# Gated mix of attention and a mixture of experts on one core: weights of the output projection fetched by another queue, and small work given other pairs of key tiles

## The chip, the cores and the metric

The kernel runs on one core of a Trainium2 chip. The core has engines that work side by side: TensorE (PE, with its weight loads shown as PEld), VectorE (DVE), ScalarE (ACT), GpSimd (POOL) and SyncE (SP, which here does nothing but issue DMAs). Each takes its instructions in order and waits on semaphores for the others. The metric is the device time of one execution in microseconds (us), less is better. "Faster" and "slower" are meant against the kernel before, on the same chip.

## The reference

One input x (2048 rows of D = 448) goes through full attention and through a mixture of experts, and a learned gate mixes the two:

```
qkv = x @ wqkv                      # 16 heads of 28
p   = softmax(q @ k.T * 28**-0.5)   # all 2048 keys, no mask
A   = (p @ v).reshape(S, D) @ wo
B   = sum over the top 2 of 8 experts of gate_e * (silu(x @ w1[e]) @ w2[e])
out = g * A + (1 - g) * B           # g per row, from gate_w
```

All is float32; the kernel computes the products of the projections and scores from two float32r parts, high and low ("h", "l"), of each factor.

## The kernel before

The projections, the router and the experts come first, until about 830 us. The rest is attention and the output projection, and only these are changed. Attention runs over 16 units. Unit u = 4g + qc takes group g of four heads and block qc of 512 queries, and goes over the keys in 8 pairs p of key tiles (128 keys each); m = 8u + p counts the pairs. For each m the code issues, in this order: `scores(m + 1)` (the scores of the next pair on TensorE, their exponentials on ScalarE), `beside(m)` (loads and small work that is spread over the pairs) and `values(m)` (P times V on TensorE).

On PE, DVE, ACT and POOL the instructions keep the order in which the code is written (`manual_schedule`). SP's queue is ordered by a scheduler, and comes out in the written order here. Of the two key tiles of a pair the scores of each fill three banks of one PSUM tile (`s0`, `s1`) and one single bank (`z0`, `z1`). The single banks are used in turn by the scores and by `values`; the last score bank of a pair is copied to SBUF by DVE (`X`, L1168), so that the bank is free again. `values` writes its result `po` into such a bank too, and DVE copies it to `osb` in pair 0 (L1185) or adds it to `osb` in the other pairs (L1187). `osb` is `accs[u]`, one tile per unit, in a pool with two buffers. Row 28 of each head's 32 rows of `osb` is the sum of the exponentials, since V carries a column of ones.

The small work beside this, with its lines before the change:

- `load_q(g, qc)` (L719, L721): 12 DMAs on SP that fetch the queries of the next unit, called in `scores(m)` where a unit begins. `load_k` (L704, L707: eight for `Kh`, four for `Kl`) and `load_v` (L691) fetch half of the keys or values of the next group; in the last unit of a group (qc = 3) they are called in pairs 3, 4 and 6, the second half of V in pair 0 of the next.
- `split_wo(b)` (L1051 to L1053): fetches block b of the output projection's weights wo into `wo_r` by a DMA of POOL and splits it on DVE into `wo_h` and `wo_l`.
- `fetch_routed(t)` and `routed(t)` (L1059, L1068 to L1072): gather the experts' rows of 128 tokens by two indirect DMAs of POOL and form the weighted sum B in four steps on DVE.
- `collect_sums(u)`, `invert_sums(u)`, `divide(u)` (L1105 to L1130): POOL sends the sums of exponentials to DRAM (`sum_d`) and fetches them back in another layout (`rc`), DVE inverts them, POOL sends them out again (`inv_d`) and spreads them over the partitions (`rs`), and DVE multiplies `osb` with them (L1120). Then SP moves the rows of `osb` to their places in `OT` (L1130): four DMAs for units 0 to 3, five for units 4 to 11 and eight for units 12 to 15.
- `split_o(t, eng)`: splits a token tile of OT into `oh` and `ol` for the output projection, which follows over 16 token tiles (`project`, `finish`).

## Time and profile before

| | us |
|---|---|
| median of 3 runs | 1383.28 (1382.78 to 1384.16) |
| the profiled execution, its time | 1384.45 |
| its span (first to last instruction) | 1382.7 |
| TensorE matmuls busy | 1348.1 (98%) |
| VectorE busy | 927.5 (67%) |
| ScalarE busy | 847.5 (61%) |
| GpSimd busy | 618.5 (45%) |

The granted clock of TensorE is 0.99 of full speed on average. The profile is one execution; its times below are counted from the start of its span. In the list of waits a row reads: engine, what it was about to write and in which line, what it waited for, the total of the waits in us, their number, the longest. A row of the timeline reads: start, duration, engine, line, operation, and in brackets the idle time before it and who ended it. SPq and POOLq are the issue of DMAs by these engines.

### The profile page before, as it was taken

The numbers are of one execution on the slowest core, as the hardware profiler recorded it, in microseconds if no ns is written. First come the engines' busy times: TensorE is split into PE (matmuls) and PEld (weight loads), VectorE is DVE, ScalarE is ACT, GpSimd is POOL, SyncE is SP. The second block draws the span as 40 slices with busy tenths as digits, with TensorE's granted clock in tenths as the row PEclk, the third lists the DMA queues.
The fourth block names the chain that finished last, engine by engine and source line by source line (L and its number), as shares of the span: only waits on it lengthen the run. The fifth ranks groups of instructions, "written<-read, shape, count | busy, mean of one in ns | idle before, by whom it ended". The sixth has DMA issues, their size and how long they took to land. (4 is left out here: it accounts for less than half of the span.)

```text
span 1382.7 us, 27175 instructions
## 1 busy us (share of the span) xinstructions
PE 1348.1 (98%) x10166; PEld 891.0 (64%) x10166; DVE 927.5 (67%) x1077; ACT 847.5 (61%) x1269; POOL 618.5 (45%) x665
## 2 busy tenths in 40 slices
PE   9999999999999999999999999999889989999998
PEld 8888788788877777777777774444333334444457
DVE  5736898888888989889887773444433444444555
ACT  5335355355344443444434349999888779999981
POOL 2114676577568675787767550222222112222220
PEclk9999999999999999999999999999999999999999
DMA  9887865653454454553445212225221322242223
GB/s 353 295 288 235 305 178 168 220 170 96 148 161 142 119 160 153 173 157 115 155 146 173 73 38 74 60 61 164 63 63 56 113 71 76 86 127 60 68 59 113
DMA packets 135958, 191.30 MB, mean 138 GB/s; under 512 B 23284, under 2 KB 102168, under 8 KB 135312
## 3 DMA queue, kind: packets, MB, share of 16 engines
q1 hardware_dynamic: 124416, 159.63, 36.7%
q0 software_dynamic: 11264, 29.68, 6.9%
q8 instruction: 80, 1.31, 0.4%
q14 instruction: 54, 0.44, 0.1%
q10 hardware_dynamic: 144, 0.23, 0.1%
HBM read 139.20 MB, written 60.74 MB: 145 GB/s over the span
## 5 line engine op out<-in xcount | busy, mean ns | idle before, releaser
L143 DVE TENSOR_REDUCE mp<-pm 128x3 f32<-128x1536 f32 (+1 forms) x301 | 508.7, 1732 | 11.0 <-PE pm L122 11.0
L1181 PE MATMUL z<-P,V 128*32 128x512 f32 x2032 | 249.4, 608 | 0.5 <-ACT P L1166 0.3
L733 PE MATMUL z<-Q,Kh 29*128 29x512 f32 x508 | 187.6, 448 | 24.4 <-DVE osb L1187 24.4
L1169 ACT ACTIVATE P<-s 128x1536 f32<-128x1536 f32 x127 | 196.2, 1545 | 22.4 <-PE s L733 22.4
L1167 ACT ACTIVATE P<-s 128x1536 f32<-128x1536 f32 x127 | 194.9, 1535 | 0.1
L1168 DVE COPY X<-z 128x512 f32<-128x512 f32 x127 | 87.8, 691 | 154.7 <-PE z L733 145.4
L733 PE MATMUL s<-Q,Kh 29*128 29x512 f32 x1524 | 189.4, 446 | 0.0
L804 POOL TENSOR_TENSOR w2l<-w2r,w2h 128x448 fp32r<-128x448 f32 x112 | 129.3, 1155 | 119.0 <-ACT w2h L798 92.4
L1020 ACT ACTIVATE yo<-acc 128x448 f32<-128x448 f32 x64 | 34.8, 544 | 233.2 <-PE acc L1006 220.5
L1006 PE MATMUL acc<-w2h,hh 128*128 128x448 f32 x448 | 167.6, 374 | 0.3 <-PEq L818 0.3
L1006 PE MATMUL acc<-w2h,hl 128*128 128x448 f32 x448 | 166.5, 372 | 0.0
L1006 PE MATMUL acc<-w2l,hh 128*128 128x448 f32 x448 | 166.1, 371 | 0.0
L733 PEld LDWEIGHTS z<-Q,Kh 29*128 29x128 f32 x508 | 75.3, 185 | 134.0 <-issue 30.5
L949 ACT ACTIVATE hf<-acc 128x512 f32<-128x512 f32 (+6 forms) x154 | 74.2, 482 | 137.9 <-PE acc L945 130.9
L136 DVE TENSOR_REDUCE mp<-acc 128x1 f32<-128x512 f32 x130 | 89.4, 688 | 87.1 <-PE pm L122 85.5
L813 POOL TENSOR_TENSOR hl<-hf,hh 128x512 fp32r<-128x512 f32 x112 | 144.9, 1294 | 1.0 <-ACT hh L952 1.0
L1105 POOL DMA_DIRECT2D sum_d<-osb x64 | 31.0, 492 | 254.5 <-DVE osb L1187 254.5
L1181 PEld LDWEIGHTS z<-P,V 128*32 128x32 f32 x2032 | 53.9, 110 | 133.3 <-issue 81.2
L945 PE MATMUL acc<-xeh,w1h 128*128 128x512 f32 (+3 forms) x408 | 136.8, 339 | 0.0
L945 PE MATMUL acc<-xeh,w1l 128*128 128x512 f32 (+3 forms) x408 | 136.0, 338 | 0.0
L1187 DVE TENSOR_TENSOR osb<-z,osb 128x512 f32<-128x512 f32 x112 | 77.4, 691 | 83.4 <-PE z L1181 81.0
L772 POOL TENSOR_TENSOR w1l<-w1r,w1h 128x1024 fp32r<-128x1024 f32 (+1 forms) x49 | 90.9, 1855 | 64.5 <-ACT w1h L766 47.8
(222 smaller groups left out, 2782.4 us busy)
## 6 DMA issues: line engine op xcount, KB each, us to landing
w2r<-in_w_dram SPq DMA_DIRECT2D x112, 224.0 KB
w1r<-in_w_dram SPq DMA_DIRECT2D x56, 384.0 KB
ys_d<-zero_d SPq DMA_DIRECT2D x32, 448.0 KB
ys_d<-yo SPq DMA_DIRECT2D x64, 224.0 KB
x_d<-xf SPq DMA_DIRECT2D x115, 64.0 KB
qkh_d<-hi SPq DMA_DIRECT2D x28, 256.0 KB
qkl_d<-lo SPq DMA_DIRECT2D x28, 256.0 KB
w1r<-in_w_dram SPq DMA_DIRECT2D x112, 64.0 KB
```

What stands on the lines that cost most here:

```text
L136: nc.vector.tensor_reduce(mp[:, o:o + 1], banks[0], axis=AX.X, op=ALU.max)
L143: nc.vector.tensor_reduce(mp[:, (o + lo) % 256:(o + lo) % 256 + hi - lo], pm[h][:, lo - 3 * h:hi - 3 * h], axis=AX.X, op=ALU.max)
L733: nc.tensor.matmul(banks[j], k[rw, ks], q[rw, c], start=i == 0, stop=i == 2)
L772: nc.gpsimd.tensor_tensor(l[:, :, half], r[:, :, half], h[:, :, half].bitcast(F32), op=ALU.subtract)
L804: nc.gpsimd.tensor_tensor(w2l, w2r, w2h.bitcast(F32), op=ALU.subtract)
L813: nc.gpsimd.tensor_tensor(hl, hf32, hh[:, 0:512].bitcast(F32), op=ALU.subtract)
L945: nc.tensor.matmul(pu[:, 0:HC], a, b[:, cs], start=i == 0, stop=i == len(mms) - 1)
L1006: nc.tensor.matmul(py[:n, 0:D], a[:, cs], b, start=i == 0, stop=i == 3 * NH - 1)
L1167: nc.scalar.activation(P[:, 1:4], t[0], AF.Exp, scale=SCALE)
L1168: nc.vector.tensor_copy(X, z[1])
L1169: nc.scalar.activation(P[:, 4:7], t[1], AF.Exp, scale=SCALE)
L1181: nc.tensor.matmul(po[32 * j:32 * j + 32], v[:, kt % 8, 32 * j:32 * j + 32], P[4 * i + j], start=i == 0, stop=i == 1)
```

## The change

The fetch of wo leaves `split_wo` and becomes `fetch_wo`, on SP, in pair 4 of units 4 to 7; the split follows in pair 0 (before: pair 1) of units 5 to 8. `collect_sums(u - 1)` is called at the beginning of `beside` for pair 0 of unit u, where it stood at the end of `values` for the last pair of unit u - 1. The gather goes from pair 0 to pair 1, the four steps of the routed rows from pairs 3, 4, 6, 7 to pairs 2, 4, 5, 6, the inversion from pair 2 to pair 3, the spreading of the inverted sums gets a function of its own in pair 4, and the division goes from pair 5 to pair 7. Of the first four tiles that `split_o` handles, three are split on DVE at other pairs of units 14 and 15, and the fourth on ACT behind the loop. In the projection's loop the spreading comes one token tile later.

```diff
+    wo_r = {}
+
+    def fetch_wo(b):
+        wo_r[b] = sb.tile([128, D], F32, name="wo_r")
+        nc.sync.dma_start(wo_r[b], wo[:, b])
+
     def split_wo(b):
-        w_ = sb.tile([128, D], F32, name="wo_r")
-        nc.gpsimd.dma_start(w_, wo[:, b])
+        w_ = wo_r[b]
         nc.vector.tensor_copy(wo_h[:, b], w_)
...
         nc.gpsimd.dma_start(by_slices(inv_d[u]), r)
+
+    def spread_sums(u):
         rs[u] = sb.tile([128, 512], F32, name="rs")
         for j in range(4):
...
             nc.vector.tensor_tensor(accs[u], po, accs[u], op=ALU.add)
-        if p == NPR - 1:
-            collect_sums(u)

     def beside(m):
...
-        if p == 0:
+        if u and p == 0:
+            collect_sums(u - 1)
+        if p == 1:
             fetch_routed(u)
-        if p == 1 and 5 <= u < 9:
+        if p == 4 and 4 <= u < 8:
+            fetch_wo(u - 4)
+        if p == 0 and 5 <= u < 9:
             split_wo(u - 5)
-        if u >= NU - 2 and p < 2:
-            split_o(2 * (u - NU + 2) + p, nc.vector)
-        if u and p == 2:
+        if (u, p) in WHOLE_O:
+            split_o(WHOLE_O.index((u, p)), nc.vector)
+        if u and p == 3:
             invert_sums(u - 1)
-        if u and p == 5:
+        if u and p == 4:
+            spread_sums(u - 1)
+        if u and p == 7:
             divide(u - 1)
-        if p in (3, 4, 6, 7):
+        if p in (2, 4, 5, 6):
             next(sums.setdefault(u, routed(u)))

+    WHOLE_O = [(NU - 2, 1), (NU - 1, 0), (NU - 1, 1)]
     for m in range(NU * NPR):
         if m + 1 < NU * NPR:
             scores(m + 1)
         beside(m)
         values(m)
+    collect_sums(NU - 1)
+    split_o(3, nc.scalar)
...
         if t == 2:
             invert_sums(NU - 1)
+        if t == 3:
+            spread_sums(NU - 1)
         if t == 5:
             divide(NU - 1)
```

The new lines shift the numbers: the X copy is L1175 after the change, the copy and the add of `osb` L1192 and L1194, the division L1127, the OT transfers L1137.

Two places show how the order moves. The first is VectorE from the division in unit 5 into unit 6. A row gives the line, the operation, out<-in with buffer numbers, and the semaphores waited for (DMAHW are lanes of SP's DMAs, DMASW those of POOL's). Before:

```order
L1120 TENSOR_TENSOR osb_11470<-osb_11470,rs_11959 128x512 [waits DMASW5_49,DMASW4_49,DMASW6_49,DMASW3_49,DMASW2_49]
L1187 TENSOR_TENSOR osb_11871<-z0_12108,osb_11871 128x512 [waits DVE_49,PE_49]
L1168 COPY X_12118<-z0_12134 128x512 [waits PE_49,Activation_49]
L1070 TENSOR_SCALAR b1_12009<-yg0_11858,coef_79 128x448
L1187 TENSOR_TENSOR osb_11871<-z1_12154,osb_11871 128x512 [waits DVE_49,PE_49]
L1168 COPY X_12177<-z1_12193 128x512 [waits PE_49,Activation_49]
L1072 SCALAR_TENSOR_TENSOR b1_12009<-yg1_11860,coef_79,b1_12009 128x448 [waits DVE_49]
L1187 TENSOR_TENSOR osb_11871<-z0_12213,osb_11871 128x512 [waits DVE_49,PE_49]
L1168 COPY X_12229<-z0_12245 128x512 [waits PE_49,Activation_49]
L1185 COPY osb_12277<-z1_12268 128x512 [waits DMAHW2_49,DMAHW6_49,DMAHW1_49,DMAHW7_49,DMAHW0_49,PE_49]
L1168 COPY X_12279<-z1_12295 128x512 [waits PE_49,Activation_49]
L1052 CAST wo_h_9776<-wo_r_12314 128x448 [waits DMASW6_49]
```

The same place after the change:

```order
L1127 TENSOR_TENSOR osb_11466<-osb_11466,rs_12053 128x512 [waits DMASW4_49,DMASW5_49,DMASW3_49,DMASW2_49]
L1194 TENSOR_TENSOR osb_11871<-z0_12215,osb_11871 128x512 [waits DVE_49,PE_49]
L1175 COPY X_12225<-z0_12241 128x512 [waits PE_49,Activation_49]
L1057 CAST wo_h_9776<-wo_r_12051 128x448 [waits DMAHW1_49]
L1058 TENSOR_TENSOR wo_l_9777<-wo_r_12051,wo_h_9776 128x448 [waits DVE_49]
L1192 COPY osb_12277<-z1_12268 128x512 [waits DMAHW5_49,DMAHW6_49,DMAHW1_49,DMAHW7_49,DMAHW0_49,PE_49]
L1175 COPY X_12279<-z1_12295 128x512 [waits PE_49,Activation_49]
L1194 TENSOR_TENSOR osb_12277<-z0_12318,osb_12277 128x512 [waits DVE_49,PE_49]
```

The division is now five rows ahead of the copy that opens unit 6, where it was nine ahead, and the split of wo stands before this copy, where it stood behind it.

The second place is SP's queue where group 1 ends and unit 8 begins (unit 7's pairs 5 to 7 and the beginning of unit 8). Before:

```order
L1130 DMA OT<-osb 16x512
L1130 DMA OT<-osb 12x512
L1130 DMA OT<-osb 28x512 x3
L704 DMA Kh_12981<-qkh_d 28x2x512
L707 DMA Kh_12981<-neg_d 1x1024
...
L704 DMA Kl_12990<-qkl_d 28x2x512 x4
L719 DMA Q<-qkh_d 28x512 x4
L719 DMA Q<-qkl_d 28x512 x4
L721 DMA Q<-m_d 1x512 x4
L691 DMA V_13106<-v_d 128x8x128
```

After the change:

```order
L704 DMA Kh_12978<-qkh_d 28x2x512
L707 DMA Kh_12978<-neg_d 1x1024
...
L704 DMA Kl_12987<-qkl_d 28x2x512 x4
L719 DMA Q<-qkh_d 28x512 x4
L719 DMA Q<-qkl_d 28x512 x4
L721 DMA Q<-m_d 1x512 x4
L1137 DMA OT<-osb 16x512
L1137 DMA OT<-osb 12x512
L1137 DMA OT<-osb 28x512 x3
L691 DMA V_13102<-v_d 128x8x128
```

The OT transfers of unit 6's rows stood ahead of the K and Q loads and now stand behind them. At the boundaries within a group the same holds without the K loads: the 12 loads of Q now come ahead of the OT transfers.

## Prediction

> **What bounds the kernel now.** I read the page's costliest groups first, then the waits after 830 us, then single rows of the engines at the places that the change touches. Everything it touches lies in attention, units 0 to 15, and the projection behind it. Two rows of the groups:
> ```profile
> L1181 PE MATMUL z<-P,V 128*32 128x512 f32 x2032 | 249.4, 608 | 0.5 <-ACT P L1166 0.3
> L1167 ACT ACTIVATE P<-s 128x1536 f32<-128x1536 f32 x127 | 194.9, 1535 | 0.1
> ```
> The last two columns are the idle time ahead of the group. TensorE and ScalarE both run these without a gap, so a delay put into this chain comes out at the end in full. The list of waits shows what delays it today:
> ```profile
> DVE wo_h L1052 <- DMA wo_r<-in_wo_dram: 27.1, 4, 7.1
> PE z L733 <- DVE osb L1187: 24.4, 4, 6.5
> ```
> Four times VectorE waits for a block of wo (27.1 us), and four times TensorE waits behind that (24.4). The copies that open a unit measure what it costs:
> ```profile
> 988.34 0.69 DVE L1185 COPY osb<-z 128x512 f32<-128x512 f32 x1 [1.18 <-PE z L1181]
> 1026.70 0.69 DVE L1185 COPY osb<-z 128x512 f32<-128x512 f32 x1 [1.18 <-PE z L1181]
> 1064.18 0.69 DVE L1185 COPY osb<-z 128x512 f32<-128x512 f32 x1 [1.18 <-PE z L1181]
> 1139.50 0.69 DVE L1185 COPY osb<-z 128x512 f32<-128x512 f32 x1 [1.17 <-PE z L1181]
> 1168.98 0.69 DVE L1185 COPY osb<-z 128x512 f32<-128x512 f32 x1 [1.17 <-PE z L1181]
> ```
> An undisturbed unit is 1168.98 - 1139.50 = 29.48 us. Units 5 to 8, those with a split of wo, take 1139.50 - 988.34 = 151.16 against 4 x 29.48 = 117.92: **33.24 us lost**. Inside one, unit 6 (37.48 us, 8.00 over):
> ```profile
> 1031.08 0.50 PE L733 MATMUL s<-Q,Kh 29*128 29x512 f32 x3
> 1037.45 0.79 PE L733 MATMUL z<-Q,Kh 29*128 29x512 f32 x1 [5.86 <-DVE osb L1187]
> 1031.08:1034.60 3.52, 0.51 (x7) 0.19 (x3) 0.00 (x0) 2.29 (x3) 0.34 (x1) 1.00 0.79 276
> 1034.60:1041.43 6.83, 3.98 (x21) 1.43 (x25) 2.47 (x5) 1.97 (x2) 0.57 (x1) 0.50 0.01 6
> 1024.83 0.69 DVE L1168 COPY X<-z 128x512 f32<-128x512 f32 x1 [1.12 <-PE z L733]
> 1028.52 0.69 DVE L1168 COPY X<-z 128x512 f32<-128x512 f32 x1 [1.12 <-PE z L733]
> 1036.71 0.68 DVE L1187 TENSOR_TENSOR osb<-z,osb 128x512 f32<-128x512 f32 x1
> ```
> The two window rows end with granted clock, DMA share and GB/s. At the boundary the add or copy follows the X copy by 1026.70 - 1024.83 = 1.87 us, so, behind the X copy of 1028.52, the add of 1036.71 was due at 1030.39: 6.32 late. The other 8.00 - 6.32 = 1.68 are the clock: after 3.5 us without matmuls it is granted at 0.50 for 6.83 us.

> **The change, part by part.** *The fetch on SP.* A block is now asked for half a unit (some 15 us) ahead of its split. The wait in VectorE was 7.1 us at its longest, so it goes: -33.2 us, clock included. The cast and subtract stand between the X copy and the copy that opens the unit, in a gap of 1.18 us of which they take about 1.03:
> ```profile
> 1035.74 0.40 DVE L1052 CAST wo_h<-wo_r 128x448 fp32r<-128x448 f32 x1 [6.53 <-DMA wo_r<-in_wo_dram]
> 1036.17 0.63 DVE L1053 TENSOR_TENSOR wo_l<-wo_r,wo_h 128x448 fp32r<-128x448 f32 x1
> ```
> Cost: 0; without that cover 4 x 1.03. SP issues four DMAs more, one per unit, some 15 us from any transfer that is waited for: 0, POOL four fewer: 0.

> *The divisions: a new wait.* This is the part that the sum hangs on. The copy that opens unit u writes an osb buffer, and there are two, so it needs the OT transfers that read unit u-2's osb to have landed. Today the division stands in pair 5 of unit u-1, now in pair 7, where today the last routed row stands (L1072, 1021.76 below). SP's queue makes it worse: there the Q loads of unit u+1 now stand ahead of the OT transfers, at units 4, 8 and 12 also eight Kh and four Kl loads. Let C be the time at which the copy was due.
> ```profile
> 1021.76 0.67 DVE L1072 SCALAR_TENSOR_TENSOR b<-yg,coef,b 128x448 f32<-128x448 f32 x1
> 860.54 1.61 SPq L719 DMA_DIRECT2D Q<-qkh_d  x4
> 863.91 1.14 SPq L721 DMA_DIRECT2D Q<-m_d  x4
> 869.86 0.69 DVE L1185 COPY osb<-z 128x512 f32<-128x512 f32 x1 [1.18 <-PE z L1181]
> 976.73 3.20 SPq L1130 DMA_DIRECT2D OT<-osb  x4
> 1015.10 3.81 SPq L1130 DMA_DIRECT2D OT<-osb  x5
> 1275.48 6.15 SPq L1130 DMA_DIRECT2D OT<-osb  x8
> 1361.16 6.16 SPq L1130 DMA_DIRECT2D OT<-osb  x8
> 1366.57 2.16 DMA OT<-osb
> 1221.03 0.50 SPq L704 DMA_DIRECT2D Kh<-qkh_d  x1
> 1228.97 1.14 SPq L721 DMA_DIRECT2D Q<-m_d  x4
> 951.01 0.50 SPq L704 DMA_DIRECT2D Kh<-qkh_d  x1
> 959.90 1.13 SPq L721 DMA_DIRECT2D Q<-m_d  x4
> ```
> The division ends where that row ends, at C - (1026.70 - 1021.76 - 0.67) = C - 4.27. The loads of Q, where nothing is ahead of them on SP (unit 1's boundary), begin at 860.54 = C - 9.32 and end at 865.05 = C - 4.81, so at an ordinary boundary they are done 0.5 us before the division and cost nothing. OT's group starts at about C - 4.23 and takes 3.20, 3.81 or 6.15 us for 4, 5 or 8 transfers. It has landed 1.41 us after its last issue ended: the tail's last issue at 1366.57 is waited for 2.16 us, to 1368.73, and the group ended at 1367.32. That gives a copy late by
> - 0.38 us at units 2, 3, 5 (4 transfers),
> - 0.99 us at units 6, 7, 9, 10, 11, 13 (5),
> - 3.33 us at units 14, 15 (8).

> At units 4, 8, 12, K and Q together take 1230.11 - 1221.03 = 9.08 us. Begun at C - 9.32, when the last scores of the old K are out, they end at C - 0.24, and OT lands at C + 4.42 (unit 4) or C + 5.03 (8 and 12). At the other end stands the slowest such group, 951.01 to 961.03, 10.02 us: 0.94 more each.

> What of a wait is lost? Unit 14 tells: its splits move the copy by about 0.08 and the next add by 0.20.
> ```profile
> 1287.17 0.69 DVE L1185 COPY osb<-z 128x512 f32<-128x512 f32 x1
> 1288.99 0.69 DVE L1168 COPY X<-z 128x512 f32<-128x512 f32 x1 [1.13 <-PE z L733]
> 1291.06 0.69 DVE L1187 TENSOR_TENSOR osb<-z,osb 128x512 f32<-128x512 f32 x1
> 1316.79 0.69 DVE L1185 COPY osb<-z 128x512 f32<-128x512 f32 x1
> ```
> The add was due at 1288.99 + 1.87 = 1290.86, and the unit takes 29.62, 0.14 over: nearly all, say the wait less 0.1. Sum of the waits: 3 x 0.28 + 6 x 0.89 + 2 x 3.23 + 4.32 + 2 x 4.93 = **26.8 us**. Bounds: all hidden, 0; with OT's landing up to 1 us later at 14 boundaries and the slow K group, about 26.8 + 14 + 2.8 = 44. I take 26.8, because each of its durations is one that these same instructions show.

> *The clock.* A boundary wait of 4.4 to 5.0 us leaves TensorE idle about 0.4 us less (6.32 late gave 5.86 idle), 4.0 to 4.6 us. The rows show a halved clock after 5.86 us of idling and say nothing of 4 to 4.6 us: bounds 0 and 3 x 1.7 = 5.1, and I take half, 2.6. [...]

> *The rest.* The add of gathered rows moves from pair 3 to pair 2:
> ```profile
> 1289.17 1.09 POOL L1059 DMA_INDIRECT yg<-ys_d,slot_i  x1 [0.30 <-issue]
> yg<-ys_d,slot_i POOLq DMA_INDIRECT x32, 4.2
> ```
> Issued at 1289.17 = C + 2.0, landed 4.2 later at C + 6.2; VectorE reaches the add at about C + 6.1 and has 0.6 us to spare. A gather slower by 1 us would cost up to 0.4 in each of 16 units, 6 us; at the median it costs 0, and a late copy widens the room, since POOL doesn't wait for it. Sums keep their order on POOL, and the transfers of inverted sums get more time than before: 0. Split_o's tile 0 leaves pair 0 of unit 14, the other two stand as before: -0.1. Tile 3 goes to ScalarE after the loop, and the OT of unit 14 comes two pairs (2 x 29.48 / 8 = 7.4 us) later, both before the tail's long wait for the last OT: 0.

> Sum: -33.2 + 26.8 + 2.6 = -3.8. The profiled execution, 1384.45 us, would become 1380.7; its time is 1.17 over the median of the runs, 1383.28, so the median becomes **1379.5**.

> **The rivals.** *The waits at the boundaries are hidden* (OT lands by C, since DMAs in the attention run faster or SP's order differs from the program's): the whole 33.2 is kept, 1350.1. Against it: today the same issues take 3.2 to 6.15 us wherever they stand, more than the 4.2 us that the new place leaves when landing is added.

> *No change.* The clock falls at all three long boundaries (+5.1) and the slow K group shows at each (+0.94 x 3 = 2.8): -33.2 + 26.8 + 5.1 + 2.8 = +1.5, 1384.8; with one of the two alone 1382.0 to 1382.3. For it: every stall of 5.9 us now brings the halved clock. Against: only the group at 951.01 was that slow.

> *Slower: Q's issue delays OT at all boundaries.* The Q group of unit 6's boundary began like this:
> ```profile
> 1019.00 2.76 SPq L719 DMA_DIRECT2D Q<-qkh_d  x4
> ```
> That is 1.15 more than at 860.54. Taken over, Q ends at C - 3.66 and OT starts 0.57 later at 11 ordinary boundaries (6.3) and 1.15 later at the other three (3.5): 1379.5 + 9.8 = 1389.3. It decides from two thirds of the boundaries on (6.6 us). For it: Q's issue was seen slow. Against it: it was slow right behind an OT group, and now nothing stands ahead of Q.

> [...]

> **How the numbers follow.** About 0.2% (2.8 us) is what a measurement of this kernel tells from no change: faster is under 1380.5, slower over 1386.1. The forecast's own range is 1377 (no halved clock) to 1382 (three): 0.50 for the case, of which 0.42 lies under 1380.5. Hidden waits: 0.07. No change by clock and K: 0.28. Slower by Q, or a landing or gather later by some 0.7 us everywhere: 0.15. Faster 0.42 + 0.07 = 0.49, same 0.08 + 0.26 = 0.34, slower 0.02 + 0.15 = 0.17. The range leaves out the hidden waits and the last of the slow cases: 1372 (a third of the boundary waits gone) to 1389.

> **What would show it.** In the changed kernel the wait for wo_r is gone from VectorE's list, and DVE osb L1192 <- DMA OT<-osb stands there, 14 times, about 27 us in all, longest 4.5 to 5.5 us, with TensorE waiting behind it. Units 5 to 8 take about 30.4 us, units 14 and 15 are opened some 3.3 us late, and units 4, 8, 12 some 4.5 to 5 us. On SP the Q loads start 9.3 us before the copy is due. I am wrong if that wait is small, if copies wait over 2 us at ordinary boundaries, or if VectorE waits for the gather at its new place.

## The result and the profile after

The changed kernel takes 1398.57 us (median of 4, 1395.46 to 1402.53) against 1383.49 before: a ratio of 1.0111 (95% interval 1.0084 to 1.0138). It is **15 us slower**; forecast were 4 us less. Its profiled execution took 1399.52 us (span 1397.7).

The list of waits after 830 us: the wait for wo is gone and the copy that opens a unit waits for OT, 14 times, as the order had said, but for twice the time that I had put there.
```profile
DVE osb L1192 <- DMA OT<-osb: 55.0, 14, 10.1
PE z L733 <- DVE osb L1192: 37.3, 14, 8.5
```
The 55.0 include what VectorE idles ahead of the copy in any case: 1.2 us, or 0.1 to 0.2 at units 5 to 8 and 15, where a split stands in this gap. Measured against the spacing of an undisturbed pair (3.685 us from add to copy) the 14 copies are late by 43.65 us together. VectorE's rows of those that open units 2, 3, 4, 8, 12, 14 and 15:
```profile
898.40 0.69 DVE L1192 COPY osb<-z 128x512 f32<-128x512 f32 x1 [1.92 <-DMA OT<-osb]
929.14 0.69 DVE L1192 COPY osb<-z 128x512 f32<-128x512 f32 x1 [2.60 <-DMA OT<-osb]
966.24 0.69 DVE L1192 COPY osb<-z 128x512 f32<-128x512 f32 x1 [8.97 <-DMA OT<-osb]
1099.46 0.69 DVE L1192 COPY osb<-z 128x512 f32<-128x512 f32 x1 [7.75 <-DMA OT<-osb]
1231.74 0.69 DVE L1192 COPY osb<-z 128x512 f32<-128x512 f32 x1 [10.09 <-DMA OT<-osb]
1297.85 0.69 DVE L1192 COPY osb<-z 128x512 f32<-128x512 f32 x1 [5.12 <-DMA OT<-osb]
1332.16 0.69 DVE L1192 COPY osb<-z 128x512 f32<-128x512 f32 x1 [3.34 <-DMA OT<-osb]
```
| copies of units | late, forecast | late, measured |
|---|---|---|
| 2, 3, 5 (4 transfers) | 0.38 each | 0.75, 1.43, 1.23 |
| 6, 7, 9, 10, 11, 13 (5) | 0.99 each | 1.51, 1.87, 1.29, 1.61, 1.23, 1.14 |
| 14, 15 (8) | 3.33 each | 3.95, 3.40 |
| 4, 8, 12 (behind K and Q) | 4.42, 5.03, 5.03 | 7.79, 7.54, 8.91 |
| sum | 28.2 | 43.65 |

The two pairs behind a copy are longer by 10.5 us in all at units 4, 7, 8, 12, 14 and 15, where the clock was halved.

In what follows I compare the length of attention, from the first copy into osb (unit 0) to the last add (unit 15): the part ahead of it, the same code in all these kernels, ended between 837.7 and 842.2 us in the profiles, which blurs totals by a few us. Before, attention takes 500.79 us, after it 519.21: +18.4, where the 33.2 of the wo stalls went and 43.65 + 10.5 came, with 2.5 us given back: the pairs behind a late copy are some 0.05 us shorter each (1.6), and what single pairs before took longer, by up to 0.3 us, is gone (0.9). The remaining -3.4 of the span's +15.0 lie ahead of attention (1.7) and in the tail (1.7).

### The profile page after: what moved, and what is told of

Read it like the earlier page. It is cut to its first block, busy times and chain, and to the rows that moved or that the text cites. A ratio compares the mean times of both kernels' runs of the same rounds, so it can differ in the third digit from the quotient of the medians.

```text
span 1397.7 us, 27189 instructions
## 1 busy us (share of the span) xinstructions
PE 1353.4 (97%) x10166; PEld 892.3 (64%) x10166; DVE 927.0 (66%) x1076; ACT 849.0 (61%) x1270; POOL 616.1 (44%) x661
## 5 line engine op out<-in xcount | busy, mean ns | idle before, releaser
L1188 PE MATMUL z<-P,V 128*32 128x512 f32 x2032 | 252.4, 615 | 0.2
L733 PE MATMUL z<-Q,Kh 29*128 29x512 f32 x508 | 188.0, 449 | 37.3 <-DVE osb L1192 37.3
L733 PE MATMUL s<-Q,Kh 29*128 29x512 f32 x1524 | 191.0, 446 | 0.0
L1175 DVE COPY X<-z 128x512 f32<-128x512 f32 x127 | 87.8, 691 | 153.8 <-PE z L733 142.2
L733 PEld LDWEIGHTS z<-Q,Kh 29*128 29x128 f32 x508 | 75.5, 185 | 152.3 <-DVE osb L1192 41.7
L1194 DVE TENSOR_TENSOR osb<-z,osb 128x512 f32<-128x512 f32 x112 | 77.4, 691 | 91.3 <-PE z L1188 91.3
```

The costliest lines, as they stand in the source:

```text
L733: nc.tensor.matmul(banks[j], k[rw, ks], q[rw, c], start=i == 0, stop=i == 2)
L1175: nc.vector.tensor_copy(X, z[1])
L1188: nc.tensor.matmul(po[32 * j:32 * j + 32], v[:, kt % 8, 32 * j:32 * j + 32], P[4 * i + j], start=i == 0, stop=i == 1)
```

## The experiments

| kernel | median us | ratio to before (95%) | attention us |
|---|---|---|---|
| changed | 1398.57 | 1.0111 (1.0084 to 1.0138) | 519.21 |
| wo fetch alone | 1351.22 | 0.9737 (0.9721 to 0.9753) | 468.06 |
| division in pair 7 alone | 1428.47 | 1.0298 (1.0281 to 1.0315) | 542.96 |
| changed, three osb buffers | 1355.53 | 0.9773 (0.9754 to 0.9791) | 472.67 |
| changed, OT first on SP | 1386.84 | 1.0003 (0.9988 to 1.0018) | 501.70 |
| changed, V later | 1399.32 | 1.0107 (1.0086 to 1.0129) | 519.03 |
| changed, gathers later | 1391.04 | 1.0050 (1.0029 to 1.0071) | 511.32 |
| changed, both later | 1392.82 | 1.0057 (1.0037 to 1.0078) | 513.59 |
| changed, division in pair 6 | 1349.38 | 0.9743 (0.9723 to 0.9763) | 471.71 |
| division 6, three buffers, routed step in pair 3 | 1346.49 | 0.9721 (0.9707 to 0.9734) | 467.30 |
| wo fetch alone, split in pair 0 | 1347.09 | 0.9724 (0.9710 to 0.9738) | 467.36 |

The runs were made in four groups, and the kernel before took 1383.49 us in the first (row 1), 1386.41 in the second (rows 2 to 5), 1383.84 in the third (rows 6 to 9) and 1385.04 in the last. The ratios are taken within a group; medians of different groups can differ by 3 us for this alone.

**The two halves of the change by themselves.** First the fetch of wo alone, on the kernel before:
```diff
-        nc.gpsimd.dma_start(w_, wo[:, b])     # in split_wo
+        nc.sync.dma_start(wo_r[b], wo[:, b])  # in fetch_wo
+        if p == 4 and 4 <= u < 8:
+            fetch_wo(u - 4)
```

> The kernel before with one edit: a block of wo is fetched by SP in pair 4 of the unit ahead, its split stays in pair 1. Theory (the early fetch is worth what the wo stalls cost, and all of the loss comes from the boundaries): 33 to 34 us faster than before, about 1350, units 5 to 8 at about 29.5 us each. Rival (part of the loss comes from the fetch, since SP's queue is held up by it): clearly above 1350, with new waits for Q or OT, 1360 or more.

Measured 1351.22, attention 32.7 us shorter, units 5 to 8 at 29.5 to 30.2 us. The gain is there in full.

Then the division alone, with wo left to POOL:
```diff
-        if u and p == 5:
+        if u and p == 7:
             divide(u - 1)
-        if p in (3, 4, 6, 7):
+        if p in (3, 4, 5, 6):
```

> The kernel before with the division alone moved: pair 7 instead of pair 5 (the routed steps in pairs 3, 4, 5, 6); wo stays with POOL. Theory (the late division alone makes the copies late, 43.7 us of lateness and 9.7 us in the pairs behind them): about 1383.5 + 53 = 1436, units 4, 8 and 12 opened 7 to 9 us late. Rival (the boundaries are late because of the other moves, such as the gather one pair later or the wo fetch in SP's queue): much less, under 1415.

Measured 1428.47, that is 42 us over the kernel before (1386.41 beside it), where 53 were expected. The mechanism is the one named: the copies are late by 45.4 us (7.2, 9.1 and 7.5 at units 4, 8, 12), attention is 42.2 us longer. The two halves do not add up to the whole exactly (-32.7 + 42.2 = +9.5, measured +18.4): attention of the changed kernel, which has the early fetch too, is only 23.8 us shorter than here. In the list of waits three of the four waits for wo are left, since at unit 8 the block has landed by the time of the late copy. Unit 8 is 0.9 us longer here than in the changed kernel, where the wait for wo cost it 8.4 before: 7.4 of the 9 us that are missing. The rest was not followed up, and the changed kernel has the other small moves besides.
```profile
DVE wo_h L1052 <- DMA wo_r<-in_wo_dram: 17.0, 3, 6.4
```

**Taking the wait away.** Three osb buffers leave every row of SP's order in its place:
```diff
-            accs[u] = sb.tile([128, 512], F32, name="osb")
+            accs[u] = sb.tile([128, 512], F32, name="osb", bufs=3)
```

> The changed kernel with three osb buffers instead of two, so that the copy into osb needs the OT transfers of three units ago; the order on every engine is the same. Theory (the loss is the wait of the copy for OT and the clock that it brings down): 53 us come back, 1345 to 1346. Rival (the bunched transfers at the boundary disturb more than the copy, such as Q or the gathers): above 1355, with other waits in place of this one.

Measured 1355.53: 46.5 us of attention come back, no copy is late and the clock is never halved in attention (0.998 was granted over the whole run). That is 10 us over the number expected and just on the rival's side of 1355: 3 lie ahead of attention in this profile, and 5.4 of attention are left against the best kernel. Other waits stand there in place of the old one, as the rival had it, but they are much smaller. With the copy no longer waiting, VectorE waits for the late OT itself, at `split_o`'s first tile in unit 14.
```profile
1262.61 0.43 DVE L1086 CAST oh<-OT 128x512 fp32r<-128x512 f32 x1 [1.81 <-DMA OT<-osb]
```
The others are waits for the gathered rows, whose first step the change has put into pair 2; they come in seven units, and lengthen pair 1 of units 4 and 12 by 1.3 and 0.9 us:
```profile
DVE yg L1073 <- DMA yg<-ys_d,slot_i: 5.9, 7, 1.9
```
The changed kernel's list has no such wait.

**Where the late landing at units 4, 8, 12 comes from: the queue.** SP's queue in written order, with OT ahead of K's second half and of Q:
```diff
-    ctx.enter_context(tc.manual_schedule(engines=MANUAL_E))
+    ctx.enter_context(tc.manual_schedule(engines=MANUAL_E | {mybir.EngineType.SP}))
...
         if u and p == 7:
             divide(u - 1)
+        if qc == 3 and g + 1 < NG and p == 7:
+            held[g + 1][0][1] = load_k(g + 1, 1)
+        if p == 7 and u + 2 < NU:
+            qs[u + 2] = load_q((u + 2) // 4, (u + 2) % 4)
```

> The changed kernel with SP's queue in written order and the loads of K's second half and of Q written behind the division, so that the OT transfers go first at every boundary. Theory (at units 4, 8 and 12 it is the queue ahead of OT): those three copies are late by 1 to 1.5 us instead of 7.5 to 8.9, without a halved clock behind them, and the other boundaries stay as they are: about 26 us less, 1372. Rival (the OT data land late there because K, Q, V and the gathers move at the same time): those three still 3 us or more late, 1378 or more.

The copies of units 4, 8 and 12 are late by 0.52, 1.03 and 1.26 us, as the queue theory says, and lateness falls from 43.65 to 21.8 us. But the total was expected at 1372 and is 1386.84: K and V, now last in the queue, arrive too late for pairs 2 to 4 of the new group, and behind the waits for them the clock is halved for 3.41 us at units 8 and 12 (TensorE was busy for 2.14 and 2.24 of the 3.41 us from 1097.46 and 1223.75 us on), where none was expected. TensorE's rows of the scores in unit 8, and the list of waits:
```profile
1099.80 0.75 PE L733 MATMUL s<-Q,Kl 28*128 28x512 f32 x2 [1.27 <-DMA Kl<-qkl_d]
```
```profile
PE z L1186 <- DMA V<-v_d: 2.3, 1, 2.3
```
Pairs there take up to 7.1 us instead of 3.7. In neither of these two orders do the transfers fit between the division and the pairs that need them.

**The landing itself.** In the changed kernel OT lands at units 4, 8 and 12 3.4 to 4.7 us behind the end of its issue; elsewhere it is 1.5 to 2.5. SP's and POOL's rows at unit 4:
```profile
951.58 3.18 SPq L704 DMA_DIRECT2D Kl<-qkl_d  x4
...
958.24 1.14 SPq L721 DMA_DIRECT2D Q<-m_d  x4
959.47 3.19 SPq L1137 DMA_DIRECT2D OT<-osb  x4
962.77 0.47 SPq L691 DMA_DIRECT2D V<-v_d  x1
```
```profile
960.51 1.02 POOL L1064 DMA_INDIRECT yg<-ys_d,slot_i  x1 [0.31 <-issue]
961.84 0.97 POOL L1064 DMA_INDIRECT yg<-ys_d,slot_i  x1 [0.30 <-issue]
```
The issue ends at 962.66 and the copy starts at 966.24. Two things move data just then: the two gathers of routed rows on POOL, and V (512 KB) right behind OT. One kernel puts V out of the way, one the gathers, a third both. V later, the main lines:
```diff
-        if g and qc == 0 and p == 0:
-            held[g][1][1] = load_v(g, 1)
...
-        if u and p == 3:
+        first = g > 0 and qc == 0
+        if u and p == (2 if first else 3):
             invert_sums(u - 1)
+            if first:
+                held[g][1][1] = load_v(g, 1, nc.gpsimd)
```
The gathers later:
```diff
-        if p == 1:
+        first = g > 0 and qc == 0
+        if p == 1 and not first:
             fetch_routed(u)
...
-        if u and p == 3:
+        if u and p == (2 if first else 3):
             invert_sums(u - 1)
+            if first:
+                fetch_routed(u)
...
-        if p in (2, 4, 5, 6):
+        if p in ((4, 5, 6, 7) if first else (2, 4, 5, 6)):
```

> The changed kernel, but at units 4, 8 and 12 the second half of V is fetched by POOL behind the inverted sums (whose inversion comes one pair earlier there), when the late copy has long been made, and no longer by SP right behind the OT transfers. Theory V (OT lands late there, 3.4 to 4.7 us behind the end of its issue, because V's 512 KB come right behind it): 1.6 us behind it as at other boundaries, about 7 us less in all, 1391. Rival (the gathers slow it, or K and Q): these three boundaries unchanged, 1398.

> The changed kernel, but at units 4, 8 and 12 the two gathers of routed rows are issued behind the inverted sums (the steps on them go to pairs 4 to 7), when the late copy has long been made; V stays behind OT on SP. Theory V: these boundaries unchanged, 1398. Rival (the gathers of 448 KB each take the time in which OT would land): OT lands 1.6 us behind its issue, about 7 us less, 1391.

> The changed kernel with both edits at units 4, 8 and 12: V and the gathers behind the inverted sums. If V or the gathers alone delay OT's landing there: 1391, as with that edit alone. If the two share it: both single edits stay at 1394 or more and this one reaches 1391. If neither does and K and Q ahead of it are the cause: 1398 still.

It is the gathers. With V later OT lands 3.54, 4.16 and 3.28 us behind its issue, as in the changed kernel, and so the earlier inversion, which both kernels have, does not matter either. Unit 4:
```profile
958.57 3.20 SPq L1137 DMA_DIRECT2D OT<-osb  x4
```
```profile
965.31 0.69 DVE L1192 COPY osb<-z 128x512 f32<-128x512 f32 x1 [8.37 <-DMA OT<-osb]
```
With the gathers later it lands 1.50, 1.51 and 1.63 us behind its issue, although V is still right behind it. Unit 4:
```profile
958.33 3.20 SPq L1137 DMA_DIRECT2D OT<-osb  x4
961.63 0.47 SPq L691 DMA_DIRECT2D V<-v_d  x1
```
```profile
963.02 0.69 DVE L1192 COPY osb<-z 128x512 f32<-128x512 f32 x1 [6.21 <-DMA OT<-osb]
```
The time is the expected 1391, attention 7.9 us shorter. Both together give 1.48, 1.50 and 1.61, no more than the gathers alone; the attention of this kernel is 2 us longer than with the gathers later alone, among others since the clock was halved at unit 3 too (TensorE was busy there for 2.00 of the 3.41 us from 927.65 us on). Whether it is the gathers' data or another part of their work that holds OT up is not shown.

**The dose.** The division one pair earlier; the last routed step makes room for it, and the scheduler puts OT ahead of all Q loads at units 4, 8 and 12, and ahead of most of them elsewhere:
```diff
-        if u and p == 7:
+        if u and p == 6:
             divide(u - 1)
-        if p in (2, 4, 5, 6):
+        if p in (2, 4, 5, 7):
```

> The changed kernel with the division in pair 6 instead of pair 7 (the last routed step in pair 7), 3.7 us earlier; the scheduler then puts the OT transfers behind K's second half but ahead of Q. Theory (lateness is the division's end plus issue and landing against the copy's due time): no copy late within groups (those were late by 1.1 to 1.9 us) and at units 14 and 15 (3.4 to 4.0) by 0 to 0.5; units 4, 8 and 12 late by 0.5 to 1.5 us, and nearly no halved clock: 1353 to 1357. Rival (it is the bunching of SP's transfers, not the deadline): still 10 us or more late in all, 1365 or more.

1349.38, 3.6 us under the range expected: lateness is 3.56 us in all, 0.59, 1.21 and 1.08 of it at units 4, 8 and 12, 0.29 and 0.35 at units 14 and 15 and none elsewhere. 3.7 us of lead, with the better place in SP's queue that comes with them, are worth 49 us. What is new since the changed kernel is a wait that the late copies of the changed kernel had covered, the gather at its place in pair 2, as with three buffers:
```profile
DVE yg L1073 <- DMA yg<-ys_d,slot_i: 5.6, 8, 1.8
```

**The best of it.** Two kernels at the end: the changed one with the division in pair 6, three buffers and the first routed step back in pair 3, and the kernel before with nothing but wo on SP, split in pair 0 (`if p == 0 and 5 <= u < 9`).

> The changed kernel with the division in pair 6, three osb buffers and the first routed step in pair 3 (routed steps in pairs 3, 4, 5, 7). In the run with the division in pair 6 alone, 3.6 us of lateness and about 2.4 us behind two waits for the gather in pair 2 were left. Theory: both go, 1349.4 less 5, 1344 to 1346. Rival (these waits only move, since TensorE and ScalarE are full): no faster than 1349.

> The kernel before with the fetch of wo by SP in pair 4 of the unit ahead and its split in pair 0 instead of pair 1; all else as before. Theory (the cast and subtract fit into VectorE's gap of 1.18 us in either pair): within 0.5 us of the run with the split in pair 1, ratio to before 0.973 to 0.975. Rival (they push the copy that opens the unit): 4 x 0.5 us or more above it.

1346.49 and 1347.09, attention 467.30 and 467.36: no difference that could be measured. The theory's 1344 to 1346 for the first was missed by half a us, and the second's ratio lies just under the expected 0.973 to 0.975 (its attention is 0.7 us shorter than with the split in pair 1). Both beat either given kernel, and the second does it with the fetch alone; all the other moves of the change, even with a third buffer, add nothing to it that can be measured.

## Why the prediction was wrong

**The wo fetch: right.** -33.2 were forecast, and the fetch alone shortens attention by 32.7, with the split in pair 0 by 33.4. Cast and subtract in pair 0 cost nothing. In the first rival this stood as 1350.1; that is about the time of each kernel here that has the early fetch and no late division.

**The divisions: the mechanism right, the size wrong.** The failed step is the sum of the waits, 26.8 us (28.2 of lateness, less 0.1 for each of 14): the copies were late by 43.65. Attention came out 22.2 us over the forecast; the waits make 15.4 of it, the clock 7.9, and 1.1 more than reckoned was given back. The sum's shape held: the division ends at C - 4.26 (forecast -4.27), and OT's issue starts at C - 4.24 at eight of the eleven boundaries within a group and takes 3.2 to 4.1 or 6.1 us. What was mis-sized:
- *The landing*, taken from the tail as 1.41 us. From the start of OT's issue to its landing 64 GB/s moved there, 42 to 63 at the boundaries within the groups and at units 14 and 15, and 154 to 176 at units 4, 8 and 12. Within the groups the landing is 1.5 to 2.5, 0.1 to 1.1 more at 11 boundaries, 5.7 us with the slower issue (lateness 19.4 against 13.7). What makes it longer there was not tested.
- *The gathers at units 4, 8 and 12.* I had put the first gather at C + 2 myself, for their own add, and never asked what flies beside them. OT, late behind K and Q, lands in the middle: 3.58, 3.42 and 4.69 us instead of 1.41, 7.5 us in all. The runs with the gathers later show this part.
- *K and Q*, forecast to end at C - 0.24: OT's issue there ended 1.20, 0.50 and 0.61 us later than forecast (at unit 4 a Kl group took 3.18 us against 1.61 at the boundary that I used), 2.3 us in all.

My upper bound of 44 for the waits held just about (43.65), by luck: it spread 14 us of later landing evenly over the boundaries and knew nothing of the gathers. It had no case of its own behind it either, and the range ended at 1389.

**The clock: wrong.** 2.6 us were forecast, at three boundaries, bound above by 5.1; it cost 10.5, at six. Two of the three longest waits halved the clock for 6.83 us and one for 10.24, and units 7, 14 and 15, of which I had expected nothing, for 3.41 each. I had read the limit off the one kind of gap that the trace before held, 5.86 us of idling, and even that row said more: the 3.52 us ahead of the halved stretch, which I called without matmuls, held 0.51 us of them, and the clock fell when TensorE had idled for 3.0 us (1031.58 to 1034.60). The lower bound of 0 for 4.0 to 4.6 us of idling had no row behind it. The windows of the changed kernel, with TensorE's busy time first and PEclk behind the engines:
```profile
1060.07:1063.48 3.41, 1.99 (x20) 0.77 (x21) 1.34 (x2) 2.99 (x4) 1.58 (x3) 1.00 0.03 2
1063.48:1066.90 3.42, 3.42 (x24) 1.39 (x20) 0.73 (x2) 1.04 (x2) 0.96 (x1) 0.50 0.78 228
1029.35:1032.76 3.41, 2.35 (x24) 0.91 (x25) 1.38 (x2) 3.34 (x5) 2.50 (x3) 1.00 0.51 108
```
At unit 7 a copy 1.87 us late left TensorE busy for 1.99 of 3.41 us, and the next window was granted half. The other window, 2.35 of 3.41 busy, had no such consequence (1.00 behind it).

**Of the rivals**, the one for slower had the right sign and the wrong place: Q's loads took 4.5 us as a rule and 5.3 to 5.5 at three boundaries, where OT began only 0.4 to 0.5 us late. What stood against the rival of hidden waits, that issue and landing together take more than the room of 4.2 us, was right: at the six boundaries with five OT issues these took 3.8 to 4.1 us together and the landing 1.5 to 2.0.

**The rest.** The moved gather add cost nothing in the changed kernel, but only because the late copies made room for it: with the division in pair 6 it waits 5.6 us, with three buffers 5.9. This is one of the signs of being wrong that the prediction named, hidden here by the larger loss. The tail is 1.7 us shorter, though not by the change: in the profiled execution before POOL paused for 2.7 us between two issues of `rs`, which happens in three of the other profiles too, whatever their code.

## What to carry to other kernels

A double-buffered tile sets a deadline for the last reader of its old content, a DMA above all; before work is moved towards that deadline, add up division, queue, issue and landing up to it, and take each with the traffic that will fly then (here 1.41 us of landing from the tail stood for 3.4 to 4.7 at units 4, 8 and 12). A transfer that slips behind its neighbours in a queue can land among others that it never met before, as OT did among the gathers. And where one part of a change brings all of the gain, try it alone first: the fetch alone was worth 2.7%, the whole change lost 1.1%.

## What the runs showed of the hardware

| windows of attention at full clock | before | changed |
|---|---|---|
| the next one halved, busy share | 4: 0.00 to 0.12 | 6: 0.00 to 0.14 (five) and 0.585 (from 1060.07 us on) |
| the next one at full clock, busy share | 134: 0.88 or more | 1: 0.579 (from 957.67 us on); 134: 0.66 or more |

In the changed kernel 1.42 us of idling in one window at unit 7 brought 3.41 us at half clock, worth 1.4 us; 1.16 us in one window at unit 10 and 1.06 us at unit 6 brought nothing. What sets the clock is not shown: no run was made that set the idle time by itself, and the windows with 0.579 and 0.585 went different ways.

**The gathers.** Two indirect gathers of 448 KB each on POOL delayed the landing of OT's transfers of up to 56 KB each on SP by 1.9 to 3.1 us (3.42 to 4.69 us behind their issue, against 1.50 to 1.63 with the gathers later), while 512 KB of V, issued on SP 0.1 us behind the OT transfers, did not.
